# Issuing the V-cache loads of a decode attention kernel from ScalarE's queue instead of SyncE's

## The chip, the cores and the metric

The kernel runs on one core of a Trainium2 chip. The metric is the device time of one launch in microseconds (us), as a median over runs. TensorE (PE), VectorE (DVE), ScalarE (ACT), GpSimd (POOL) and SyncE (SP) each work through an instruction stream of their own, in order, and meet at semaphores. A transfer is started by an instruction in one of these streams and then carried by 16 DMA engines. In the profile of this kernel all loads, which SyncE issues, go through one queue (q1); the core's instructions come through two others (q8 and q14).

## What is computed

One decode step (a single new token in each of 8 batch rows) of attention over a cached K and V, with a small MLP beside it, on the same normalised input:

```python
def _A_ref(x, k_cache, v_cache, wq, wo):          # 8 batch rows, 32 heads, 4096 keys, 128 wide
    q = (x @ wq).reshape(B, 1, 32, 128).transpose(0, 2, 1, 3)
    scores = jnp.einsum("bhqd,bhkd->bhqk", q, k_cache) * (128 ** -0.5)
    p = _softmax(scores, axis=-1)
    o = jnp.einsum("bhqk,bhkd->bhqd", p, v_cache)
    return o.transpose(0, 2, 1, 3).reshape(B, 1, 4096) @ wo

def _B_ref(x, w1, b1, w2, b2):
    h = _gelu(_layernorm(x) @ w1 + b1)
    return h @ w2 + b2

xn = _layernorm(x)
return x + _A_ref(xn, ...) + _B_ref(xn, ...)
```

Everything is bf16. The two caches hold 268 MB each and every byte of them is read once, so the kernel moves about 552 MB from HBM.

## The kernel before

**Tiling.** The 32 heads are taken in 8 groups of 4 (`HS`), and with 8 batch rows that makes 64 steps (`NQ`), numbered `i = hq * 8 + b`. Step i needs one 4096 KB block of K and one 4096 KB block of V. In SBUF a block is a tile of 128 partitions x 128 keys x 128 values: partition p holds 128 consecutive keys of one head. `K_sb` and `V_sb` have two slots each (index `i % 2`).

**One step.** Of the 128 keys of a partition, 88 are scored on VectorE in four chunks of 22 (`dve_chunk`, three instructions each: multiply with the broadcast query `qbc_sb`, add halves, reduce). The other 40 go over TensorE in five batches of 8: transpose (`pe_T`), eviction by ScalarE (`act_T`), a small matmul with the query (`pe_QK`); ScalarE then copies these scores beside VectorE's (`act_S`). `dve_max` finds the maximum in five short instructions, of which the first writes `mx_sb`; `act_exp` makes the probabilities in four activations. `pe_PV` multiplies them with V in 8 groups of 4 matmuls, `act_E` evicts and normalises the result, `pe_ex` spreads it into its place. After 8 steps `pe_oproj` applies `wo`.

**Order.** The program is first written down as a list: `at(position, function, arguments)`. The list is sorted by position, and the functions are called in that order; each call appends instructions to the streams of the engines it names. A position therefore sets the order within every engine, not a time. Step i has its base at `o = i * 100`. Its K scoring lies between o+5 and o+92, its `dve_max` and `act_exp` at o+100 and o+106, its `pe_PV` between o+122 and o+185, between the `pe_T` and `pe_QK` of step i+1. `act_E` of step i is at o+193.

**Loads.** All transfers are issued by SyncE, in the order of the list. Ahead of everything: x, wq, b2, K(0) in four pieces, K(1), V(0) (positions -900 to -850). `load_mlp` at 20 waits until all of the query projection is done with `W_sb` and then loads the MLP weights into the same tile; `load_wo` at 201 waits for the last MLP matmul (`tk["mlp"]`), for the same reason. `load_k(i)` (L239) stands at o-90 and waits until step i-2 is through with its K slot: its last transposes (`kt`) and VectorE's last multiply (`km`). `load_v(i)` (L248) stands at o+20, so between `load_k(i+1)` at o+10 and `load_k(i+2)` at o+110, and waits for `tk[("pv", i - 2)]`, the last PV matmul of step i-2. SyncE's order in the long run is thus K(i+1), V(i), K(i+2), V(i+1), and so on. V(2) stands behind `load_wo` and K(3). The last V block is loaded in four pieces. Each slot has semaphores of its own.

`act` and `sp` in the code record the instruction streams of ScalarE and SyncE. All instructions carry the line of a helper, L99, so they are told apart by their tiles.

Of the kernel before, what the change touches and what calls it, by code (L numbers as in the profile page):

```python
# [103 lines left out]
def bass_parallel_sum__gqa_block_cached__mixer_channel_mlp__decode_kernel(  # L104
# [41 lines left out]
    with ExitStack() as es:  # L146
# [61 lines left out]
        pe, dve, act, sp, pool = (_Eng(sem(f"{n}_s")) for n in ("pe", "dve", "act", "sp", "pool"))  # L208
        NPIECE = 4
        ld_k = [[_Dma(sem(f"ld_k{s}_{q}")) for q in range(NPIECE)] for s in range(2)]  # L210
        ld_v = [[_Dma(sem(f"ld_v{s}_{q}")) for q in range(NPIECE)] for s in range(2)]
# [3 lines left out]
        tk = {}  # L215
        prog = []

        def at(pos, fn, *a):
            prog.append((pos, len(prog), fn, a))
# [14 lines left out]
        def cache_src(cache, i, lo, hi):  # L234
            hq, b = divmod(i, B)
            return cache[b, hq * HS:(hq + 1) * HS].rearrange(
                "h (p j) d -> (h p) j d", j=NKEY)[:, lo:hi, :]
# [10 lines left out]
        def load_v(i):  # L248
            s, n = i % 2, (NPIECE if i == NQ - 1 else 1)
            if i >= 2:  # L250
                sp.wait(tk[("pv", i - 2)])
            for q in range(n):
                lo, hi = q * NKEY // n, (q + 1) * NKEY // n
                tk[("v", i, q)] = ld_v[s][q].sig(sp.dma_start(
                    V_sb[:, s, lo:hi, :], cache_src(A_v_cache, i, lo, hi)))

        def load_mlp():
# [328 lines left out]
        at(-870, load_k, 0)  # L586
        at(-860, load_k, 1)
        at(-850, load_v, 0)
        at(-800, consts_pool)
        at(-790, norm, 0)  # L590
# [19 lines left out]
        for i in range(NQ):  # L610
            o = i * Q
            hq, b = divmod(i, B)
            if i >= 2:
                at(o - 90, load_k, i)
            if i >= 1:
                at(o + 20, load_v, i)
            if b == 4 and hq + 1 < NHQ:
                at(o + 50, qrep, hq + 1)
                at(o + Q + 50, qbc, hq + 1, 0)
                at(o + Q + 60, qbc, hq + 1, 1)  # L620
            for t in range(NT):
                at(o + 5 + 14 * t, pe_T, i, t)
                at(o + 10 + 14 * t, act_T, i, t)
                at(o + 26 + 14 * t, pe_QK, i, t)
            at(o + 92, act_S, i)
            for c in range(NCH):
                at(o + 10 + 22 * c, dve_chunk, i, c)
            at(o + Q, dve_max, i)
            at(o + Q + 6, act_exp, i)
            at(o + Q + 20, pe_RS, i)  # L630
            at(o + Q + 25, dve_rinv, i)
            for g in range(NPVG):
                at(o + Q + 22 + 9 * g, pe_PV, i, g)
            at(o + Q + 93, act_E, i)
            at(o + 2 * Q + 12, pe_ex, i)
            if b == B - 1:
                at(o + 2 * Q + 14, cp_o, hq)
                at(o + 2 * Q + 30, pe_oproj, hq)
# [56 lines left out]
```

## Time and profile before

| | |
|---|---|
| median of 3 runs | 1320.73 us (1317.72 to 1322.85) |
| profiled execution | 1317.31 us, of it the profiled span 1315.5 us |
| mean granted TensorE clock | 0.843 |
| HBM read | 551.80 MB, 419 GB/s over the span |
| VectorE busy | 1118.8 us (85% of the span) |
| TensorE matmul busy | 951.0 us (72%) |
| ScalarE busy | 553.2 us (42%) |
| transfers of V | 63 of 4096 KB and 4 of 1024 KB |
| transfers of K | 62 of 4096 KB and 8 of 1024 KB |

The span is what the hardware profiler saw between the first and the last instruction of one execution; 1.8 us lie around it. "PE MATMUL PV_ps<-V_sb,P_sb" is one group of instructions: a TensorE matmul that writes the tile `PV_ps` and reads `V_sb` and `P_sb`. "SPq" is SyncE's stream of DMA instructions; the time beside such an instruction is what it takes to issue, and the landing is counted from its start until the semaphore tells that all the data is there. The DMA share of a window is the mean busy share of the 16 DMA engines; it can read a little above 1 in short windows. "mean granted clock" is the share of TensorE's clock that the power throttle allowed.

### The profile page before, as it was taken

The numbers are of one execution on the slowest core, as the hardware profiler recorded it, in microseconds if no ns is written. First come the engines' busy times: TensorE is split into PE (matmuls) and PEld (weight loads), VectorE is DVE, ScalarE is ACT, GpSimd is POOL, SyncE is SP. The second block draws the span as 40 slices with busy tenths as digits, with TensorE's granted clock in tenths as the row PEclk, the third lists the DMA queues.
The fourth block names the chain that finished last, engine by engine and source line by source line (L and its number), as shares of the span: only waits on it lengthen the run. The fifth ranks groups of instructions, "written<-read, shape, count | busy, mean of one in ns | idle before, by whom it ended". The sixth has DMA issues, their size and how long they took to land.

```text
span 1315.5 us, 19126 instructions
## 1 busy us (share of the span) xinstructions
PE 951.0 (72%) x8116; PEld 441.2 (34%) x8116; DVE 1118.8 (85%) x1180; ACT 553.2 (42%) x1177; POOL 11.8 (1%) x23
## 2 busy tenths in 40 slices
PE   3765876876777776777776777687786787686686
PEld 2432333333333332333333333333332333343232
DVE  3857898898899889898898898888898888988885
ACT  1343444444444434434534434434533434444443
POOL 1000000000000000000000000000000000000000
PEclk9887878888878978877887888887887887888888
DMA  9999999999999999999999999999999999999993
GB/s 397 422 403 430 434 431 428 430 433 429 429 429 433 430 428 432 431 430 429 429 430 431 423 430 427 431 431 427 425 431 433 426 430 429 432 429 422 431 413 143
DMA packets 24474, 553.03 MB, mean 420 GB/s; under 512 B 2291, under 2 KB 6468, under 8 KB 6469
## 3 DMA queue, kind: packets, MB, share of 16 engines
q1 hardware_dynamic: 24388, 551.81, 98.2%
q8 instruction: 63, 1.03, 0.3%
q14 instruction: 23, 0.18, 0.0%
HBM read 551.80 MB, written 0.01 MB: 419 GB/s over the span
## 4 chain that ended last, share of the span: by engine, by line
DMA 65%; PE 32%; DVE 1%; ACT 1%; issue 0%; SPq 0%; ACTq 0%
DMA V_sb<-in_A_v_cache_dram 63%; PE PV_ps L99 23%; PE TR_ps L99 5%; PE S_ps L99 4%; DMA K_sb<-in_A_k_cache_dram 2%; DVE Y_sb L99 1%; DVE Sd_sb L99 0%; ACT KT_sb L99 0%; PE CH_ps L99 0%; PE ACC_ps L99 0%; ACT qbc_sb L99 0%; SPq L99 0%; ACT P_sb L99 0%; ACT Sd_sb L99 0%; ACT E_sb L99 0%
## 5 line engine op out<-in xcount | busy, mean ns | idle before, releaser
L99 PE MATMUL PV_ps<-V_sb,P_sb 128*16 128x512 bf16 x2048 | 641.1, 445 | 173.1 <-DMA V_sb<-in_A_v_cache_dram 173.1
L99 ACT ACTIVATE KT_sb<-TR_ps 128x1024 bf16<-128x1024 bf16 x320 | 320.7, 1022 | 559.4 <-PE TR_ps L99 557.7
L99 DVE TENSOR_REDUCE Sd_sb<-Y_sb 128x22 f32<-128x1408 bf16 x256 | 414.7, 1620 | 8.7
L99 DVE TENSOR_TENSOR Y_sb<-K_sb,qbc_sb 128x2816 bf16<-128x2816 bf16 x256 | 410.2, 1603 | 9.5 <-DMA K_sb<-in_A_k_cache_dram 9.5
L99 PEld LDWEIGHTS PV_ps<-V_sb,P_sb 128*16 128x16 bf16 x2048 | 156.7, 96 | 385.8 <-DMA V_sb<-in_A_v_cache_dram 178.6
L99 DVE TENSOR_TENSOR Y_sb<-Y_sb 128x1408 bf16<-128x1408 bf16 x256 | 229.1, 895 | 8.8
L99 PE MATMUL TR_ps<-ident_bf,K_sb 128*128 128x128 bf16 x2560 | 217.5, 234 | 15.9 <-DMA K_sb<-in_A_k_cache_dram 15.9
L99 PEld LDWEIGHTS TR_ps<-ident_bf,K_sb 128*128 128x128 bf16 x2560 | 160.4, 104 | 118.6 <-issue 100.6
L99 PEld LDWEIGHTS S_ps<-qT_sb,KT_sb 128*128 128x128 bf16 x2560 | 89.1, 98 | 164.6 <-issue 148.5
L99 DVE TENSOR_REDUCE mx_sb<-Sd_sb 128x1 f32<-128x128 f32 x64 | 18.3, 286 | 123.5 <-ACT Sd_sb L99 123.4
L99 ACT ACTIVATE P_sb<-Sd_sb,NB_sb 32x128 bf16<-32x128 f32 x256 | 102.0, 398 | 40.6 <-DVE NB_sb L99 38.2
L99 PE MATMUL S_ps<-qT_sb,KT_sb 128*128 128x4 bf16 x2560 | 117.8, 170 | 1.5 <-ACT KT_sb L99 1.4
L99 PE MATMUL CH_ps<-rs_sb,mask_sb 128*16 128x1 f32 x128 | 12.9, 170 | 131.6 <-ACT P_sb L99 103.1
L99 ACT ACTIVATE Sd_sb<-S_ps 32x40 f32<-32x40 f32 x256 | 49.7, 194 | 100.4 <-PE S_ps L99 98.1
L99 PEld LDWEIGHTS CH_ps<-rs_sb,mask_sb 128*16 128x16 f32 x128 | 7.4, 96 | 142.5 <-ACT P_sb L99 112.9
L99 ACT ACTIVATE E_sb<-PV_ps,rinv_sb 16x512 bf16<-16x512 f32 x64 | 43.4, 677 | 16.7 <-PE PV_ps L99 7.3
L99 ACT ACTIVATION_READ_ACCUMULATOR P_sb<-Sd_sb,NB_sb 32x1 f32 x256 | 47.0, 184 | 0.0
L99 PE MATMUL CH_ps<-ident_bf,E_sb 16*128 16x4 bf16 x256 | 15.9, 163 | 18.5 <-ACT E_sb L99 18.5
L99 ACT ACTIVATE qbc_sb<-TR_ps 128x512 bf16<-128x512 f32 x16 | 9.4, 597 | 32.8 <-PE TR_ps L99 32.8
L99 PEld LDWEIGHTS CH_ps<-ident_bf,E_sb 16*128 16x128 bf16 x256 | 10.3, 91 | 30.2 <-ACT E_sb L99 30.0
L99 PE MATMUL CH_ps<-xT_sb,W_sb 128*128 128x8 bf16 (+1 forms) x230 | 11.0, 179 | 11.3 <-DMA W_sb<-in_A_wq_dram 11.2
L99 POOL COPY qrep_sb<-qT_sb 128x1024 bf16<-128x1024 bf16 x8 | 9.6, 1206 | 932.5 <-PE TR_ps L99 906.5
(55 smaller groups left out, 123.8 us busy)
## 6 DMA issues: line engine op xcount, KB each, us to landing
V_sb<-in_A_v_cache_dram SPq DMA_DIRECT2D x63, 4096.0 KB, 26.2
K_sb<-in_A_k_cache_dram SPq DMA_DIRECT2D x62, 4096.0 KB, 19.6
K_sb<-in_A_k_cache_dram SPq DMA_DIRECT2D x8, 1024.0 KB, 17.7
W_sb<-in_A_wq_dram SPq DMA_DIRECT2D x1, 5120.0 KB, 15.2
W_sb<-in_A_wo_dram SPq DMA_DIRECT2D x1, 5120.0 KB, 23.3
V_sb<-in_A_v_cache_dram SPq DMA_DIRECT2D x4, 1024.0 KB, 11.4
W_sb<-in_B_w_dram SPq DMA_DIRECT2D x1, 2160.0 KB, 21.7
W_sb<-in_B_w_dram SPq DMA_DIRECT2D x1, 2080.0 KB, 26.5
```

Source lines behind the costliest of these rows:

```text
L99: inst = getattr(e, name)(*a, **k)
```

## The change

`load_v` is recorded on ScalarE's stream instead of SyncE's: both its wait for the PV matmuls of step i-2 and its DMA instructions. Its position moves from o+20 to o-6, directly behind `act_E` of step i-2 (at o-7) and ahead of `act_exp` of step i-1 (at o+6). V(0) keeps position -850; on ScalarE's stream it is the first instruction of all. V(1) stands at 94, behind `act_S` of step 0. K and the weights stay on SyncE.

```diff
         def load_v(i):
             s, n = i % 2, (NPIECE if i == NQ - 1 else 1)
             if i >= 2:
-                sp.wait(tk[("pv", i - 2)])
+                act.wait(tk[("pv", i - 2)])
             for q in range(n):
                 lo, hi = q * NKEY // n, (q + 1) * NKEY // n
-                tk[("v", i, q)] = ld_v[s][q].sig(sp.dma_start(
+                tk[("v", i, q)] = ld_v[s][q].sig(act.dma_start(
                     V_sb[:, s, lo:hi, :], cache_src(A_v_cache, i, lo, hi)))
@@
             if i >= 2:
                 at(o - 90, load_k, i)
             if i >= 1:
-                at(o + 20, load_v, i)
+                at(o - 6, load_v, i)
```

The streams of TensorE, VectorE and GpSimd are the same instruction for instruction. ScalarE's stream gains 67 DMA instructions, SyncE's loses them.

## The prediction

> **What bounds the kernel now.** I read the page's slices first, then the chain of waits, then SyncE's own timeline.
>
> ```profile
> DMA  9999999999999999999999999999999999999993
> GB/s 397 422 403 430 434 431 428 430 433 429 429 429 433 430 428 432 431 430 429 429 430 431 423 430 427 431 431 427 425 431 433 426 430 429 432 429 422 431 413 143
> q1 hardware_dynamic: 24388, 551.81, 98.2%
> DMA 65%; PE 32%; DVE 1%; ACT 1%; issue 0%; SPq 0%; ACTq 0%
> ```
>
> The DMA engines are busy in every slice but the last, at about 430 GB/s, nearly all of it on one queue. The chain is V transfer, PV matmuls, V transfer; but that is only the order in which buffers come free. Bytes at 430 GB/s set the pace: 4096 KB are 4.194 MB, or 9.75 us, so a K and a V block cost 19.5 us a step. Only time in which the DMA engines have nothing to do, or a changed rate, can move the total.
>
> ```profile
> 610.09 0.33 SPq L99 DMA_DIRECT2D K_sb<-in_A_k_cache_dram  x1
> 613.27 0.33 SPq L99 DMA_DIRECT2D V_sb<-in_A_v_cache_dram  x1
> 630.58 0.33 SPq L99 DMA_DIRECT2D K_sb<-in_A_k_cache_dram  x1
> 634.06 0.33 SPq L99 DMA_DIRECT2D V_sb<-in_A_v_cache_dram  x1
> ...
> K_sb<-in_A_k_cache_dram SPq DMA_DIRECT2D x62, 4096.0 KB, 19.6
> V_sb<-in_A_v_cache_dram SPq DMA_DIRECT2D x63, 4096.0 KB, 26.2
> ...
> PE PV_ps L99 <- DMA V_sb<-in_A_v_cache_dram: 173.1, 61, 7.4
> ```
>
> A K block lands 19.6 us after issue although it needs 9.75: about 10 us of queue are always ahead of it. A mean is had from the end: the last K is issued at 1257.50, and the window from there to the end moved 256 GB/s x 58.5 us = 15.0 MB. Less three blocks (K(63), V(62), V(63): 12.6 MB) that leaves 2.4 MB, a backlog of 5.6 us. V is what comes just in time (TensorE waits 2.8 us a step for it).
>
> **The change, part by part.**
>
> *Issue cost.* 67 DMA instructions of 0.33 us leave SyncE, which idles, and join ScalarE: 22 us of issue in all, before the exponentials of each step.
>
> ```profile
> 614.00 0.24 DVE L99 TENSOR_SCALAR mb_sb<-nsc_sb,mq_sb 128x32 f32<-128x32 f32 x1
> 614.53 0.40 ACT L99 ACTIVATE P_sb<-Sd_sb,NB_sb 32x128 bf16<-32x128 f32 x1 [0.51 <-DVE NB_sb L99]
> ```
>
> ScalarE waits 0.51 us for VectorE exactly there, so 0.33 us fit: nothing. With that cover gone, TensorE's 2.8 us wait for V would hide it still; without either it is 62 x 0.33 = 20 us. The four pieces of V(63) (the four K pieces took 1.75 us to issue) exceed the gap by 1.2 us once, under a V wait of 2.6 us: nothing.
>
> *The wait.* `act_E` of step i-2, one place ahead, already waits for the same PV matmuls, so the new wait on ScalarE adds nothing, and the exponentials and evictions behind it lose nothing. V leaves 0.8 us later than from SyncE (eviction 0.68 plus gaps). K(i+2) no longer stands behind V(i), but its own slot comes free some 17 us later: nothing gained.
>
> *The start.* Here the order changes. On SyncE, V(0) stood behind x, wq, b2, K(0) and K(1); V(2) behind `load_wo` and K(3).
>
> ```profile
> 0.74 0.39 SPq L99 DMA_DIRECT2D x_sb<-in_A_x_dram  x1
> 1.19 0.36 SPq L99 DMA_DIRECT2D W_sb<-in_A_wq_dram  x1
> ...
> 4.47 0.49 SPq L99 DMA_DIRECT2D V_sb<-in_A_v_cache_dram  x1
> ...
> 67.74 0.38 SPq L99 DMA_DIRECT2D W_sb<-in_A_wo_dram  x1
> 68.29 15.78 SPq L99 DMA_DIRECT2D K_sb<-in_A_k_cache_dram  x1
> 84.12 0.43 SPq L99 DMA_DIRECT2D V_sb<-in_A_v_cache_dram  x1
> ...
> 100.77 1.04 PE L99 MATMUL TR_ps<-ident_bf,K_sb 128*128 128x128 bf16 x8 [10.81 <-DMA K_sb<-in_A_k_cache_dram]
> ```
>
> V(0) now leaves at about 0.74, ahead of wq (1.19). Whether its 9.75 us go first or alternate with wq (12.2 us), wq and K(0) end 9.75 us later, and so does the start of all arithmetic. The bounds are 0 (SyncE's queue goes first) and 9.75; served in order of issue, the nearest row, it is 9.75, and I take that. By itself this costs nothing, since the DMA engines carry V(0) meanwhile. It costs where a load waits for arithmetic: `load_wo` moves from 67.7 to 77.5. All that was issued before it ends with V(1), which landed at 76.6, data end 74.8 (landing trails the data by 1.8: wq's 5.24 MB, from 2.4 us on, end at 14.6 and land at 16.4). The engines idle 77.5 - 74.8 = 2.7 us.
>
> Then wo (5.24 MB at the 363 GB/s of that stretch, 14.4 us) and V(2) run until 77.5 + 24.2 = 101.7. V(3) is issued behind PV of step 1: 90.0 + 9.75 + 0.8 = 100.5. K(3), issued earlier on SyncE behind wo, now shares with V(3). In order of issue K(3) is first and lands at 101.7 + 9.75 + 1.8 = 113.3. If the queues alternate, it ends after both, at 121.2, and lands at 123.0 (before: 100.7). No row has two full queues. The nearest one is the instruction queue: 63 packets came through q8 while q1 had some 10 us queued, and no engine is shown waiting for instructions. A second queue is thus served in between, so I take 123.0 and keep 113.3.
>
> With 123.0: VectorE's last multiply of K(3) ends 14.0 us after it starts (100.75 to 114.76), so K(5) is issued at 137.0. K(4) ended at 121.2 + 9.75 = 131.0, and V(4) needs PV of step 2, which waited for K(3)'s transposes (124.9 + 13.4). The engines idle 6.0 us. Sum of the start: 8.7 us. With 113.3: K(5) at 127.3, no idling, 2.7 us.
>
> *The long run.* When both queues hold work, V's rest and the new K run at half rate. V must still land 9.8 us after the K issue (now 1257.50 to 1267.3) or TensorE delays everything; 9.8 less some 4 us of landing and spread leaves 5.8 us at half rate, a backlog of 2.9 instead of 5.6. K, all at half rate, takes 19.5 + 4 = 23.5 us and may take 24.2 (one period of 19.6 plus 3.4 from issue to the maximum plus 1.2 to the chunk). So the pace stays the DMA's, but each issue comes 2.7 us later against the bytes moved, and the end, which is arithmetic after the last K, moves by as much. Bounds: 0 if order of issue holds, 5.6 with no backlog left; I take 2.5.
>
> Sum: 8.7 + 2.5 = 11.2 us. On the profiled execution, 1317.3 + 11.2 = 1328.5; that one lies 3.4 below the median, from which it is 1331.9. I say 1330.
>
> *Two rules of the Trainium skill.* "DMA: Bandwidth & Descriptors", section "Issuing engines are not separate DMA queues", speaks against the change: transfers of several issuers run on the same 16 engines, so more issuers save only issue time. The slices above, full with one queue, agree; by the rule alone the gain is zero and the time 1317.3. The same page, "Queues, rings and completion order", says that an engine goes round-robin between queue rows, packet by packet. No row here shows two full queues; by it K(3) lands at 123.0, in strict order of issue at 113.3, which is 1328.5 against 1320.0.
>
> **The rivals.**
>
> *Order of issue is kept* across both queues: only the 2.7 us at `load_wo`, 1317.3 + 2.7 = 1320, on the median 1323. For it: both queues end in the same engines. Against it: q8's packets. 18%.
>
> *Not slower: a second queue raises the rate.* Over 150 to 1250 us the mean is 429 GB/s, the best slice 434, 1.2% more, or 13 us over 1100 us. 1317.3 + 11.2 - 13 = 1315; without the start's loss, 1304. It decides from a steady 433 on. Against it: the engines already read busy throughout. Or SyncE's queue is served first and V(0) costs nothing: 1317 to 1320. 15%.
>
> *The long run starves.* A backlog of 2.9 us is little: K issues vary by 0.9 us about 19.6, and landings trail the mean by 2.3 (9.8 - 5.6 - 1.8). If single engines run dry for 0.25 us in each of 60 steps: 15 us more, 1343.5, on the median 1347. Against it: a shorter backlog also lets K and V land earlier. 14%.
>
> **How the numbers follow.** Forecast 53%, rivals 18, 15 and 14. The forecast's own range is 1322 to 1338 (start 2.7 to 12, backlog 0 to 5.6). The range reaches to the starving case and to the unchanged one: 1317 to 1346. 0.5% (6.6 us) is about what a measurement of this kernel can tell from no change. Slower by more: most of the forecast, all of the starving case and little of the others, 0.66. Within: the order-of-issue case and the forecast's lower end, 0.23. Faster: 0.11.
>
> **What would show it.** Right: V(0) issued first and wq landing near 26; `load_wo` near 77; TensorE's first transpose of K(3) near 123; two stretches below full DMA share before 140 us, 429 GB/s afterwards; K landing 20 to 23 us after issue, V below 26. Wrong: K still landing in order ahead of a later V; a K(3) near 113; a rate of 433 or 425 in the long run; ScalarE held in a DMA instruction for longer than 0.5 us, which I cost at nothing.

## The result, and the profile after

| | before | after |
|---|---|---|
| median | 1319.26 us (1317.72 to 1322.85, 4 runs) | 1333.51 us (1332.87 to 1335.29, 4 runs) |
| profiled execution | 1317.31 us, span 1315.5 | 1335.29 us, span 1333.2 |
| mean granted TensorE clock | 0.843 | 0.819 |

The ratio is 1.0101, with a 95% interval of 1.0084 to 1.0118: slower by 1.0%, or 13.3 us on 1319.26. Three larger sets of runs of the kernel before (15 to 19 each, timed with the experiments) have medians of 1320.65 to 1321.42; against these it is 12.1 to 12.9 us. The two profiled executions lie at opposite ends of the scatter and are 17.7 us apart in span, so what is counted in the profiles below has to come to 17.7, not 13.3.

The page of the kernel after, slices, queues, chain and DMA issues (tile, stream, count, KB each, median us to landing):

```profile
DMA  9999899999999999999999999999999999999991
GB/s 399 429 358 398 361 437 427 418 432 433 429 428 430 427 431 428 435 428 428 426 430 431 430 429 428 428 429 429 426 433 428 430 429 431 424 425 437 425 424 67
...
q1 hardware_dynamic: 14740, 283.37, 50.1%
q10 hardware_dynamic: 9648, 268.44, 47.0%
...
DMA 62%; PE 30%; DVE 6%; ACT 1%; issue 0%; SPq 0%; ACTq 0%; DVEq 0%
...
V_sb<-in_A_v_cache_dram ACTq DMA_DIRECT2D x63, 4096.0 KB, 25.8
K_sb<-in_A_k_cache_dram SPq DMA_DIRECT2D x62, 4096.0 KB, 24.7
...
W_sb<-in_A_wq_dram SPq DMA_DIRECT2D x1, 5120.0 KB, 24.0
W_sb<-in_A_wo_dram SPq DMA_DIRECT2D x1, 5120.0 KB, 37.6
```

The same bytes now come through two queues, half and half. The middle is what it was, about 429 GB/s. What is new stands at the left, in the third to the fifth slice (358, 398 and 361 GB/s; before 403, 430 and 434), and at the right, in the last slice (67 GB/s; before 143): the last bytes come in some 25 us before the end of the span, where it was some 19. Landings are longer: K 24.7 us instead of 19.6, wq 24.0 instead of 15.2, wo 37.6 instead of 23.3.

TensorE's longest waits after (engine, tile, for what: us in total, times, longest):

```profile
PE TR_ps L99 <- DMA K_sb<-in_A_k_cache_dram: 264.2, 62, 25.6
PE PV_ps L99 <- DMA V_sb<-in_A_v_cache_dram: 31.0, 25, 3.4
```

K, not V, is now the load that comes just in time; V's 173.1 us of waits have become 31.0, and K's 15.9 have become 264.2. This alone costs nothing while the DMA engines stay full: e9_best_two below has 196.7 us of waits for K and is as fast as the kernel before.

The start, from the timelines of ScalarE's and SyncE's DMA instructions, and TensorE's first transpose of K(3):

```profile
0.74 0.39 ACTq L99 DMA_DIRECT2D V_sb<-in_A_v_cache_dram  x1
...
1.19 0.36 SPq L99 DMA_DIRECT2D W_sb<-in_A_wq_dram  x1
...
75.89 0.39 SPq L99 DMA_DIRECT2D W_sb<-in_A_wo_dram  x1
...
123.26 1.04 PE L99 MATMUL TR_ps<-ident_bf,K_sb 128*128 128x128 bf16 x8 [25.59 <-DMA K_sb<-in_A_k_cache_dram]
```

And stretches of time (start:end, length, busy time of each engine, clock, DMA share, GB/s), first before, then after:

```profile
70.00:80.00 10.00, 6.64 (x52) 2.78 (x50) 8.06 (x12) 6.64 (x16) 0.00 (x0) 0.77 0.96 364
130.00:140.00 10.00, 10.00 (x81) 4.22 (x80) 9.83 (x8) 3.07 (x3) 0.00 (x0) 0.83 1.00 428
150.00:1250.00 1100.00, 815.48 (x6816) 369.82 (x6815) 974.32 (x1017) 478.51 (x1022) 6.24 (x6) 0.84 1.00 429
...
70.00:80.00 10.00, 10.00 (x131) 5.10 (x128) 0.19 (x1) 2.90 (x7) 0.00 (x0) 0.83 0.69 256
130.00:140.00 10.00, 8.64 (x90) 4.37 (x88) 9.76 (x8) 3.88 (x8) 0.00 (x0) 1.00 0.21 67
150.00:1260.00 1110.00, 829.48 (x6880) 396.59 (x6878) 992.85 (x1029) 490.41 (x1039) 6.24 (x6) 0.82 1.00 429
```

V(0) leaves beside x, ahead of wq; wq lands at 25.2 (before 16.4), `load_wo` is issued at 75.9 (before 67.7), and K(3) is there at 123.3 (before 100.8). Two holes open, at 70 to 80 and at 130 to 140; against 429 GB/s they are worth 10 x (429 - 256)/429 = 4.0 us and 10 x (429 - 67)/429 = 8.4 us. The kernel before isn't full from 70 to 80 either (364 GB/s, while it loads wo), so against it the first hole is 10 x (364 - 256)/429 = 2.5 us. From 150 on the rate is 429 GB/s, as before.

That two full queues share is seen directly in the queues' part for 626 to 642 us (packets, MB, share of the engines' time):

```profile
q1 hardware_dynamic: 118, 3.51, 51.5%
q10 hardware_dynamic: 119, 3.38, 49.1%
```

The packets come one for one. This is what the Trainium skill's page "DMA: Bandwidth & Descriptors", section "Queues, rings and completion order", says of queue rows, and the packet counts agree.

### The profile page after: what moved, and what is told of

It reads as the page before. It is cut to its first block, busy times and chain, and to the rows that moved or that the text cites. A ratio compares the mean times of both kernels' runs of the same rounds, so it can differ in the third digit from the quotient of the medians.

```text
span 1333.2 us, 19126 instructions
## 1 busy us (share of the span) xinstructions
PE 957.3 (72%) x8116; PEld 464.9 (35%) x8116; DVE 1126.8 (85%) x1180; ACT 557.9 (42%) x1177; POOL 11.8 (1%) x23
## 4 chain that ended last, share of the span: by engine, by line
DMA 62%; PE 30%; DVE 6%; ACT 1%; issue 0%; SPq 0%; ACTq 0%; DVEq 0%
DMA V_sb<-in_A_v_cache_dram 38%; DMA K_sb<-in_A_k_cache_dram 24%; PE PV_ps L99 21%; PE TR_ps L99 5%; DVE Y_sb L99 3%; PE S_ps L99 3%; DVE Sd_sb L99 2%; PE CH_ps L99 1%; PE ACC_ps L99 1%; ACT KT_sb L99 0%; ACT qbc_sb L99 0%; SPq L99 0%; ACT P_sb L99 0%; DVE oTn_sb L99 0%; ACT E_sb L99 0%
## 5 line engine op out<-in xcount | busy, mean ns | idle before, releaser
L99 PE MATMUL PV_ps<-V_sb,P_sb 128*16 128x512 bf16 x2048 | 618.5, 432 | 32.6 <-DMA V_sb<-in_A_v_cache_dram 31.0
L99 ACT ACTIVATE KT_sb<-TR_ps 128x1024 bf16<-128x1024 bf16 x320 | 325.4, 1023 | 477.2 <-PE TR_ps L99 470.2
L99 PE MATMUL TR_ps<-ident_bf,K_sb 128*128 128x128 bf16 x2560 | 250.9, 257 | 264.2 <-DMA K_sb<-in_A_k_cache_dram 264.2
L99 PEld LDWEIGHTS TR_ps<-ident_bf,K_sb 128*128 128x128 bf16 x2560 | 186.1, 115 | 362.1 <-DMA K_sb<-in_A_k_cache_dram 294.6
## 6 DMA issues: line engine op xcount, KB each, us to landing
V_sb<-in_A_v_cache_dram ACTq DMA_DIRECT2D x63, 4096.0 KB, 25.8
K_sb<-in_A_k_cache_dram SPq DMA_DIRECT2D x62, 4096.0 KB, 24.7
W_sb<-in_A_wo_dram SPq DMA_DIRECT2D x1, 5120.0 KB, 37.6
W_sb<-in_B_w_dram SPq DMA_DIRECT2D x1, 2160.0 KB, 16.5
```

The lines of the kernel that those rows point to most:

```text
L99: inst = getattr(e, name)(*a, **k)
```

## The experiments

They differ from the kernels before and after only in which stream issues a load and at what place. In most of them `load_v` chooses its stream by the block's number, with SyncE's blocks at their old place:

```diff
-            if i >= 2:
-                act.wait(tk[("pv", i - 2)])
+            q_eng = sp if i < 4 else act
+            if i >= 2:
+                q_eng.wait(tk[("pv", i - 2)])
...
-                tk[("v", i, q)] = ld_v[s][q].sig(act.dma_start(
+                tk[("v", i, q)] = ld_v[s][q].sig(q_eng.dma_start(
...
-                at(o - 6, load_v, i)
+                at(o + 20 if i < 4 else o - 6, load_v, i)
```

### e1_start_sp: the start undone

The edit above: V(0) to V(3) as before the change, the rest as after it.

> V(0) to V(3) are issued from SyncE at their old places, V(4) to V(63) from ScalarE as changed. Theory (the loss sits in the order of the first loads and, smaller, of the last ones; the long run on two queues is free): the two idle stretches before 140 us, 12 us together, are gone, the end stays longer by 5 to 7 us; about 1325 us, between 1322 and 1328. Rival (two queues cost something in every step): 1330 or more, with a rate below 429 GB/s or gaps between 200 and 1250 us. Rival (all of it is the start): 1318 to 1321.

1323.91 us, ratio to the kernel before 1.0026 (1.0016 to 1.0035). No hole: 0 to 160 us moves the same 66.6 MB as before. So the start is the larger part, 1.0101 - 1.0026 = 0.75% or 9.9 us. The last 0.26% sits elsewhere, and the trace of this kernel shows where. K(63) is issued at 1260.63, 3.1 us later than before (1257.50), and its last piece, for which TensorE waits, lands some 30 us after that issue (some 20 before). Timeline of TensorE and VectorE in e1_start_sp:

```profile
1285.54 1.04 PE L99 MATMUL TR_ps<-ident_bf,K_sb 128*128 128x128 bf16 x8 [5.89 <-DMA K_sb<-in_A_k_cache_dram]
...
1290.52 1.04 PE L99 MATMUL TR_ps<-ident_bf,K_sb 128*128 128x128 bf16 x8 [3.75 <-DMA K_sb<-in_A_k_cache_dram]
...
1305.39 0.21 DVE L99 STREAM_TRANSPOSE NB_sb<-mb_sb 128x32 f32<-128x32 f32 x1
```

`NB_sb` is the last number of step 63's maximum, after which only the last softmax, PV and the projection are left: it is a good mark of the end, and stood at 1300.49 before.

### e4_start_end_sp: the end undone too

V(0) to V(3) and V(61) to V(63) on SyncE (`i < 4 or i >= NQ - 3`); 57 of the 64 V blocks stay on ScalarE.

> V(0) to V(3) and V(61) to V(63) are issued from SyncE at their old places, the 57 between from ScalarE as changed. Theory (long run free): K(63) lands about 21 us after issue instead of 31, and the time is that of before within 3 us, 1318 to 1322. Rival (two queues cost something in every step, or the smaller backlog is what the end pays for): 1325 or more.

1320.76 us, 0.9999 (0.9989 to 1.0008). Timeline of e4_start_end_sp:

```profile
1260.77 1.75 SPq L99 DMA_DIRECT2D K_sb<-in_A_k_cache_dram  x4
1262.57 19.43 SPq L99 DMA_DIRECT2D V_sb<-in_A_v_cache_dram  x5
...
1301.26 0.21 DVE L99 STREAM_TRANSPOSE NB_sb<-mb_sb 128x32 f32<-128x32 f32 x1
```

K(63) is issued just as late as in e1_start_sp, but V(62) stands behind it in the same queue, TensorE has no wait for K there, and the end is at 1301.26, 0.8 after that of the kernel before. So the late issue of K costs almost nothing by itself, since fewer bytes are then ahead of it. What costs at the end is that the last K, which the closing arithmetic waits for, shares the engines with V(62). And 57 blocks on ScalarE, with their issue and their wait, cost nothing.

### e2_v0_sp: only V(0) put back

> V(0) alone is issued from SyncE at its old place, all others from ScalarE as changed. Theory: the first idle stretch (4 us, wo waiting for late arithmetic) goes, K(3) still stands behind wo, V(2) and V(3) and lands near 120 us, so the second one (8 us) stays: 1329 us, between 1327 and 1332. Rival (everything comes from V(0) ahead of wq): both stretches go, 1322 to 1326.

1335.46 us, 1.0116 (1.0099 to 1.0133): missed by 6 us. wq lands after 15.1 us, so the first delay is gone, but V(1) now leaves ScalarE at 35.98 and shares with the MLP weights. DMA issues, SyncE's timeline and two stretches of e2_v0_sp, one fence each:

```profile
W_sb<-in_B_w_dram SPq DMA_DIRECT2D x1, 2160.0 KB, 31.4
```

```profile
76.91 0.39 SPq L99 DMA_DIRECT2D W_sb<-in_A_wo_dram  x1
```

```profile
70.00:80.00 10.00, 10.00 (x137) 5.47 (x136) 0.00 (x0) 2.05 (x3) 0.00 (x0) 0.80 0.60 230
130.00:140.00 10.00, 9.42 (x94) 4.65 (x92) 9.83 (x8) 4.53 (x8) 0.00 (x0) 1.00 0.32 113
```

That piece of the MLP weights takes 31.4 us (16.5 after, 21.7 before), TensorE's first matmul with it starts at 61.27 (59.92 after, 51.65 before), `load_wo` comes as late as in the changed kernel, and both holes are back. The delay is not V(0)'s alone: V(1) beside the MLP weights makes it as well.

### e3_wo_late: wo moved out of the start

```diff
-        at(201, load_wo)
+        at(612, load_wo)
```

> As the changed kernel, but wo is loaded later, behind K(7) on SyncE, so that K(3) to K(7) stand behind neither the MLP nor wo; V(0) still goes first. Theory: both idle stretches need wo ahead of K(3); without it 12 us are gone and the end's 5 to 7 us stay: 1325 us, between 1320 and 1328, although wq still lands near 25 us. Rival (V(0) ahead of wq is the cause): K stays 10 us behind and 1330 or more is left.

1335.19 us, 1.0109 (1.0094 to 1.0124): missed by 10 us. Stretches, DMA issue, and VectorE's wait in e3_wo_late:

```profile
70.00:80.00 10.00, 10.00 (x129) 5.05 (x128) 0.09 (x1) 2.83 (x6) 0.00 (x0) 0.82 0.70 274
...
200.00:1250.00 1050.00, 787.20 (x6426) 365.85 (x6426) 926.21 (x954) 452.25 (x953) 9.22 (x5) 0.79 1.00 426
```

```profile
W_sb<-in_A_wo_dram SPq DMA_DIRECT2D x1, 5120.0 KB, 58.6
```

```profile
221.26 1.62 DVE L99 TENSOR_TENSOR Y_sb<-K_sb,qbc_sb 128x2816 bf16<-128x2816 bf16 x1 [25.63 <-DMA K_sb<-in_A_k_cache_dram]
```

The first hole stays although no wo is issued there: K(3) itself waits for step 1's transposes, which are late by the same shift. The second hole has only moved: wo, now issued at 152.9, takes 58.6 us, the K block behind it in SyncE's queue lands at 221, and from 230 to 240 the engines move 160 GB/s, which is 6.3 us. Over the whole long run it is 426 instead of 429 GB/s, (429 - 426)/429 x 1050 = 7.3 us.

### e7_v01_sp and e8_v01_sp_wo_act: the two holes one by one

e7_v01_sp has V(0) and V(1) on SyncE (`i < 2`).

> V(0) and V(1) are issued from SyncE at their old places, the others from ScalarE as changed; wo stays on SyncE ahead of K(3). Theory (a V that alternates with weights, or with a K behind them, delays these): the weights come as before, so the first stretch is gone; wo (landing over 35 us after issue instead of 23) and K(3) still share with V(2) and V(3), K(3) lands near 120 us, and the second stretch (7 to 8 us) stays: 1331, between 1328 and 1334. Rival (the second stretch follows from the first): 1322 to 1326.

1332.32 us, 1.0085 (1.007 to 1.01). The first hole is gone (427 GB/s over 60 to 80 us), the second is there (260 GB/s over 120 to 140), because wo on SyncE shares with V(2) and then V(3) (48 packets of each queue from 100 to 104 us) and holds up K(3) behind it, which TensorE sees at 120.5.

e8_v01_sp_wo_act adds one edit: `load_wo` goes behind V(2) on ScalarE, so that K(3) has SyncE's queue to itself.

```diff
-            sp.wait(tk["mlp"])
-            tk["wo"] = ld_wo.sig(sp.dma_start(wo_sb, A_wo.rearrange("(h p) n -> p h n", p=P)))
+            act.wait(tk["mlp"])
+            tk["wo"] = ld_wo.sig(act.dma_start(wo_sb, A_wo.rearrange("(h p) n -> p h n", p=P)))
```

> As the kernel before it in this list, but wo is issued from ScalarE behind V(2), so that no K stands behind it. Theory: K(3) lands before 100 us, no stretch without transfers, only the end's 3 us stay: 1320 to 1325. Rival (V in the way of K(3) is enough, wo doesn't matter): 1328 or more.

1323.81 us, 1.0021 (1.0012 to 1.0031). TensorE's first transpose of K(3) in e8_v01_sp_wo_act:

```profile
96.32 1.04 PE L99 MATMUL TR_ps<-ident_bf,K_sb 128*128 128x128 bf16 x8 [5.42 <-DMA K_sb<-in_A_k_cache_dram]
```

No hole is left and all of the start is regained, with 62 V blocks on ScalarE. wo takes 47.9 us, and no engine waits for it.

### e6_queue_only and e5_place_only: the queue and the place apart

e6_queue_only keeps ScalarE's stream but the old place (`at(o + 20, load_v, i)`).

> Only the queue is changed: V is issued from ScalarE at its old place o+20, behind the first K-transpose eviction of step i and the exponentials, some 6 us later than in the changed kernel; V(0) is still the first transfer of all. Theory: the first idle stretch (near 75 us) stays; V(3) is issued only after K(3) has landed, so K(3) stands behind wo and V(2) but not V(3), lands near 112 us, and the second stretch shrinks or goes: 1322 to 1331. Rival (the immediate issue behind the eviction is what makes the loss): 1320 or less.

1323.88 us, 1.0018 (1.0009 to 1.0028). V(0) still goes first and the first hole stays (248 GB/s over 70 to 80), but V(3) is issued at 115.0, when K(3) has already landed (113.9), and there is no second hole. ScalarE's DMA instruction and TensorE's first transpose of K(3) in e6_queue_only:

```profile
115.02 0.33 ACTq L99 DMA_DIRECT2D V_sb<-in_A_v_cache_dram  x1
...
113.94 1.03 PE L99 MATMUL TR_ps<-ident_bf,K_sb 128*128 128x128 bf16 x8 [17.55 <-DMA K_sb<-in_A_k_cache_dram]
```

K(3) stands behind wo here too, and comes 17.6 us later than in e8_v01_sp_wo_act (96.32). So wo ahead of K(3) does not make the second hole by itself; V(3) has to come in ahead of K(3) or beside it.

e5_place_only is the kernel before with `load_v` at o-6 on SyncE: one queue, with V(i) ahead of K(i+1).

> Only the place in the order is changed: V(i) stands at o-6 on SyncE, so K and V still share one queue, but V(i) is issued ahead of K(i+1) and V(2) ahead of wo. Theory (two queues, not the new place, make the start's idle stretches): no stretch without transfers before 150 us, and wo lands some 24 us after issue or sooner. K(i+1) is held back 3.5 us by the wait for PV and lands behind a whole V block, so the backlog shrinks and K comes just in time; the end pays as in the changed kernel: 1321 to 1329. Rival (the place is what costs, on any queue): 1331 or more.

1341.07 us, 1.0146 (1.0131 to 1.0161): slower than the whole change, and missed by 12 us and more. The start has no hole; the long run does. Stretches of e5_place_only, and SyncE's timeline:

```profile
200.00:1250.00 1050.00, 747.46 (x6378) 362.14 (x6377) 918.91 (x954) 453.58 (x963) 5.28 (x5) 0.82 0.99 421
...
244.00:248.00 4.00, 3.29 (x28) 1.24 (x26) 2.52 (x5) 2.26 (x6) 0.00 (x0) 1.00 0.42 176
```

```profile
222.82 0.33 SPq L99 DMA_DIRECT2D V_sb<-in_A_v_cache_dram  x1
223.24 0.38 SPq L99 DMA_DIRECT2D K_sb<-in_A_k_cache_dram  x1
247.32 0.33 SPq L99 DMA_DIRECT2D V_sb<-in_A_v_cache_dram  x1
247.69 0.43 SPq L99 DMA_DIRECT2D K_sb<-in_A_k_cache_dram  x1
```

At the end of a group of 8 steps, where `pe_oproj` stands between the PV matmuls, the wait for PV ends late: 24.5 us from one V issue to the next instead of 19.5. K stands behind that wait on SyncE and is late as well, and the DMA engines run dry. Among windows of 4 us from 200 to 1250, ten are under 340 GB/s, at 244, 404, 464, 564, 568, 724, 884, 1044, 1104 and 1204, that is, one or two at the end of every group (160 us) and two elsewhere (464 and 1104); together they lack 17.4 us, out of (429 - 421)/429 x 1050 = 19.6. In the kernel after there is one such window (1.2 us). There the group's end is late for V in the same way, but K is free of it. The two streams in the kernel after:

```profile
253.80 0.33 SPq L99 DMA_DIRECT2D K_sb<-in_A_k_cache_dram  x1
257.36 0.34 ACTq L99 DMA_DIRECT2D V_sb<-in_A_v_cache_dram  x1
```

So the second queue does have a use: it lets K pass V's wait, and makes the new place harmless in the long run, which it is not on SyncE.

### e9_best_two: the best version that the runs suggest

e8_v01_sp_wo_act with V(61) to V(63) on SyncE as well.

> Two queues with the order repaired: V(0), V(1) and V(61) to V(63) from SyncE at their old places, wo from ScalarE behind V(2), all other V from ScalarE. Theory: nothing is lost at either end, and wo's 4096 small packets run beside large ones: 1316 to 1321, at most 3 us below the kernel before. Rival (wo on ScalarE's queue only moves the hole to V(3)): 1323 or more.

1319.76 us, 0.9994 (0.9985 to 1.0002): not to be told from the kernel before. No version here beats it.

### e10_before_wo_act: a small load on the second queue

The kernel before, with `load_wo` alone on ScalarE.

> The kernel before with one load moved: wo is issued from ScalarE, so K(3) and V(2) no longer wait for the MLP on SyncE and wo's small packets (363 GB/s when alone, 2 us more than at 430) alternate with large ones. Theory: 1 to 3 us less than before, 1317 to 1320; the end's arithmetic is unchanged. Rival (the second queue only delays what shares with it): no less than before, or more.

1333.55 us, 1.0099 (1.0084 to 1.0115): missed by 14 us. DMA issues, TensorE's timeline, the queues from 80 to 240 us, and two stretches of e10_before_wo_act:

```profile
W_sb<-in_A_wo_dram ACTq DMA_DIRECT2D x1, 5120.0 KB, 175.0
```

```profile
248.07 0.69 PE L99 MATMUL ACC_ps<-oTn_sb,W_sb 128*128 128x8 bf16 x20 [24.33 <-DMA W_sb<-in_A_wo_dram]
```

```profile
q1 hardware_dynamic: 2227, 64.69, 94.4%
q10 hardware_dynamic: 2501, 3.20, 5.6%
```

```profile
225.00:250.00 25.00, 1.93 (x24) 0.99 (x24) 7.98 (x6) 0.00 (x0) 0.00 (x0) 0.50 0.82 329
250.00:275.00 25.00, 22.73 (x214) 11.07 (x213) 15.01 (x17) 12.95 (x26) 0.00 (x0) 0.97 0.74 307
```

Packet for packet the two queues are served about alike (2227 and 2501), but wo's packets hold 3.20 MB / 2501 = 1280 B and those of K and V over twenty times as much. wo gets 5.6% of the engines' time and lands 175 us after issue, and the first output projection waits 24 us for it. TensorE stands still meanwhile, no buffer comes free, and the two stretches lack 25 x (100 + 122)/429 = 12.9 us, about what this kernel is slower by. Before, in SyncE's queue, wo had its turn and took 23.3 us.

## Why the prediction was right, point by point

1330 us with a range of 1317 to 1346 was said, slower the likeliest; it is 1333.5. An account of all kernels with the long run at 429 GB/s shows how well the parts add up. "Short at the start" is what the eight windows of 20 us from 0 to 160 moved less than those of the kernel before (66.66 MB), divided by 429 GB/s. "End mark" is the last `NB_sb`, less 1300.49.

| kernel | short at the start, us | V(62) shares with K(63) | end mark, us | ratio |
|---|---|---|---|---|
| after | 10.4 | yes | +16.0 | 1.0101 |
| e2_v0_sp | 11.6 | yes | +15.0 | 1.0116 |
| e7_v01_sp | 8.0 | yes | +13.1 | 1.0085 |
| e6_queue_only | 3.1 | in part (V(62) 6.7 us behind) | +4.9 | 1.0018 |
| e1_start_sp | 0.1 | yes | +4.9 | 1.0026 |
| e8_v01_sp_wo_act | 0.0 | yes | +4.7 | 1.0021 |
| e4_start_end_sp | 0.0 | no | +0.8 | 0.9999 |
| e9_best_two | 0.1 | no | -0.1 | 0.9994 |

The end mark is the shortage at the start plus 4.8 us (the mean of e1 and e8) where V(62) shares with K(63): 15.2 for the kernel after, where 16.0 is measured. The other kernels with a yes come out within 1.4 us (e2_v0_sp, 16.4 against 15.0, is the worst). The rest of the 17.7 us between the spans is the last 32 PV matmuls, 8.75 us instead of 7.07.

*Issue cost, nothing; the wait, nothing.* Both hold: e4_start_end_sp and e9_best_two have 57 and 59 V blocks on ScalarE and are as fast as before. The DMA instructions of V took 0.33 to 0.39 us there, under the 0.5 that I named as the limit, with one exception: in e9_best_two V(3), issued right behind wo, held ScalarE for 22.49 us, and even that cost nothing that can be seen. In the kernel after, the last four pieces took 2.16 us together and the slowest of them 0.54.

*V(0) ahead of wq, +9.75 us.* The size holds, a little smaller: wq 8.8 us later, `load_wo` 8.2 us later (75.9, predicted 77.5). The way I took there does not: V(0) needs 9.75 us but landed 21.5 us after issue, shortly ahead of wq (24.0), so the two shared and did not go in order of issue. I had said that both ways give the same delay.

*Two queues alternate, K(3) near 123.* Holds: 123.26 against 123.0. The rival in which the order of issue is kept would have had 113, and it falls, also by the packet counts of 118 and 119. That it fits to 0.3 us is partly luck: `load_wo` came 1.6 us earlier than in my sum, which from there gives 121.4.

*The start's sum, 8.7 us.* The mechanism is right and the size is low. Against the kernel before, the first hole is worth 3.1 us over 60 to 80 (399 and 332 GB/s), where I had 2.7, and the second 8.2 over 120 to 140 (429 and 253 GB/s), where I had 6.0; the other six windows give back 0.9, which makes 10.4. So the second hole is the term that was too small. Part of that I left out: I let the hole end with the issue, at 137.0, but V(4), issued at 137.40, moves nothing before 138 (0 GB/s from 137 to 138, 492 from 138 to 139). The rest was not followed up. Two things were missing from the step. It is not only `load_wo` that waits for the late arithmetic but K(3) too (e3_wo_late), and V(1) beside the MLP weights delays it as much as V(0) ahead of wq does (e2_v0_sp). The two holes cost nearly independently of each other: with the first gone, 8.0 of 10.4 us remain (e7_v01_sp), and with only the second gone, 3.1 (e6_queue_only), 11.1 together.

*The long run: pace unchanged, K later, end later by 2.5 us.* The pace holds (429 GB/s), so the rival of a starving long run (1343.5) falls, and so does that of a higher rate. K's landing is 24.7 us, above the 20 to 23 I gave, and V's 25.8 is below 26 as said. The failed step is "each issue comes 2.7 us later against the bytes moved, and the end, which is arithmetic after the last K, moves by as much". The issue did come 3.1 to 3.3 us later, but e4_start_end_sp shows that this is given back when K(63) is not shared. What moves the end is the order of the last transfers: V(62) takes half of the engines while K(63) comes in. It costs 4.8 us by the end mark, and (1.0026 - 0.9999) x 1320 = 3.6 us by the medians. That the 2.5 came near in size is luck: the cause is one that I hadn't seen.

*Which rule.* The Trainium skill's section "Issuing engines are not separate DMA queues" ("DMA: Bandwidth & Descriptors") has more issuers save issue time only. The rate agrees with it, 429 GB/s with one queue and with two; the 1.0% comes from the order in which bytes arrive, of which that sum (1317.3) takes no account.

## What to carry to other kernels

When the DMA engines are already full, a second queue adds no bytes (429 GB/s here with one and with two); it takes away an order. Go through the places where one load is needed before another (weights at the start, the last block before a closing chain, loads in small packets) and keep those loads ahead in one queue; a second queue is worth having where a load would otherwise stand behind another load's wait, as K behind V's in e5_place_only. Here that only made a new place harmless; no version with two queues was faster than the kernel before. Check a moved issue by what is at the head of the other queue at that moment, not by its place in the program.

## What the runs showed of the hardware that I had not expected

Sharing goes by packets and not by bytes, and how hard that can hit a load: wo, 5120 KB in packets of 1280 B, landed after 23.3 us in the one queue of the kernel before, after 37.6 (after) and 58.6 us (e3_wo_late) beside a second busy queue, and after 175.0 us (e10_before_wo_act) when it stood alone in its queue against one that held K and V all the time. The load that was issued right behind it held up its issuing engine: K(3) on SyncE took 15.78 us to issue in the kernel before, and V(3) on ScalarE 22.49 us in e9_best_two. Why is not shown.

ScalarE's timeline in e9_best_two:

```profile
90.80 22.49 ACTq L99 DMA_DIRECT2D V_sb<-in_A_v_cache_dram  x1
```

And the clock at the end can account for part of the scatter of a kernel's runs. The last 32 PV matmuls, which nothing hides, took 7.07 us at a granted clock of 1.00 (before, and e9_best_two), 8.75 at 0.80 (after) and 9.92 at 0.71 (e4_start_end_sp): 2.85 us between executions of the same instructions. The runs of the kernel before lie 5.1 us apart (1317.72 to 1322.85); as only one execution of each kernel has a trace, how much of that is the clock is not shown.
